# The first layer's output stored from ScalarE's own DMA queue, and the second half of the last block's output copied into a borrowed buffer

## The chip, the cores and the metric

The kernel runs on one core of one Trainium2 chip, the other cores idle. The metric is the device time of one execution in microseconds (us), taken as the median of several runs. The core's engines are TensorE (PE, with its weight loads shown apart as PEld), VectorE (DVE), ScalarE (ACT), GpSimd (POOL, unused here) and SyncE (SP), each with its own instruction queue, and 16 DMA engines that serve the transfers that SP and ACT issue.

## The reference, cut to what matters

```python
def reference(q, k, v, p, moe_w_in, moe_w_out, moe2_w_in, moe2_w_out):
    # attention in two steps; batch 8, heads 8, sequence 576, head size 64, 32 packed rows p
    p_packed = sm_attn(p, k, v)
    out = sm_attn(q, p_packed, p_packed)
    x = out.transpose(0, 2, 1, 3).reshape(4608, 512)
    h = x @ moe_w_in                    # 512 -> 2048
    g = h * np.tanh(softplus(h))        # "Mish"
    y = g @ moe_w_out                   # 2048 -> 512, the first layer's output
    h = y @ moe2_w_in
    g = h - np.tanh(h)
    return g @ moe2_w_out
```

## The kernel before, in words

The 4608 tokens are worked in nine blocks of 512. Block b (0 to 7) holds the last 512 tokens of batch b, and the ninth block ("the rest block", number 8) collects the 64 tokens left over from each of the eight batches. Attention and the first matrix of the first layer are folded together per batch, so for each batch a transposed attention matrix (tiles `a2`, four buffers, two per batch) is multiplied with a per-batch weight (tiles `m`). This gives the inner values of one of 16 feature blocks in a PSUM bank (`bk`, line 821). ACT applies Mish (L826), ACT and DVE split the result into two fp32r halves (L803, L804), and PE multiplies it with the outer weights `wo` into four accumulators (L783). The four accumulators `acc` 0 to 3 are the four blocks of 128 output features, each 128 features by 512 tokens, and every accumulator collects over the 16 feature blocks.

When a block is finished, the function `outputs` empties the accumulators: ACT copies accumulators 0 and 1 into the two halves of a buffer `yv` (L793), a DMA on SP's queue stores it to `y_d` in DRAM (512 KB), and then accumulators 2 and 3 go the same way. There is one buffer `yv`, so the second pair's copy waits until the first pair's store has landed. The next block's sums for an accumulator start only after its copy.

The second layer multiplies by a seven-product scheme for 2x2 blocks (Strassen-Winograd). It works on "supers" of two token blocks each (0 to 3, with super 4 being the rest block alone). `combos` loads the stored `y_d` blocks of a super, forms seven combinations on ACT and DVE (L920, L925, L926) and stores them to `yq_d`. For super 3, which needs block 7, this happens late, through small `x` and `xw` buffers. `load_sup` loads the combinations `yq` of a super back: of seven pairs the first two pairs (four loads of 512 KB) go to the four `a2` buffers, the others to `wo` buffers. `products` makes the seven products for each pair p of feature blocks in `bk` banks (L1047); ACT copies (L1067) and DVE adds (L1072) combine them. `second` computes h - tanh(h) on ACT and DVE (L1104 to L1121, working in the same six `xw` buffers), and PE accumulates the output with L1132.

No order is written out by hand. Every operation is an `Op` with an engine, an assumed duration, a key, the operations that it depends on, and the buffers that it takes and gives back. `Plan.emit` walks a simulated time. Whenever an engine is free it issues the ready operation with the lowest key whose buffers are free. An operation on the pseudo-engine `NONE` issues no instruction. For most kinds of buffer a queue is kept in the order of the keys, and a buffer goes to an operation only when that operation stands at the head of its kind's queue; `a2` is one of these kinds. The order of every engine's instructions therefore depends on these numbers throughout, but is fixed when the program is built.

Of the kernel before, what the change touches and what calls it, by code (L numbers as in the profile page):

```python
# [12 lines left out]
AF = mybir.ActivationFunctionType  # L13
# [5 lines left out]
B, H, S, D, P = 8, 8, 576, 64, 32  # L19
# [3 lines left out]
TB = 512  # L23
# [13 lines left out]
def r(ap):  # L37
    return ap.bitcast(F32R)
# [33 lines left out]
class Plan:  # L72
# [12 lines left out]
    def op(self, eng, dur, fn, key, deps=(), take=(), give=(), table=None):  # L85
        o = Op()
        o.table = table
        o.eng, o.dur, o.fn, o.key = eng, dur, fn, key
        o.takes, o.gives, o.outs, o.ready, o.end = list(take), list(give), [], 0.0, None
        o.wait = 0  # L90
        o.seq = len(self.ops)
        for b in o.gives:
            b.left += 1
        for d in set(x for x in deps if x is not None):
            d.outs.append(o)
            o.wait += 1
        self.ops.append(o)
        return o
# [19 lines left out]
    def emit(self):  # L118
# [3 lines left out]
        free = {e: 0.0 for e in engs}  # L122
# [13 lines left out]
        t, left = 0.0, len(self.ops)  # L136
        while left:
# [7 lines left out]
            while moved:  # L145
                moved = False
                for e in engs:
                    if free[e] > t:
                        continue
                    while pend[e] and pend[e][0][0] <= t:  # L150
                        o = heapq.heappop(pend[e])[2]
# [34 lines left out]
                    o = pick  # L186
# [9 lines left out]
                    if e == "SP":  # L196
                        free[e] = t + 0.475
                        dma_free = max(dma_free, free[e] + 0.65) + o.dur
                        o.end = dma_free + 1.6
                    else:  # L200
                        dur = o.dur
                        if o.table is not None:
                            dur += self.TABLE * (o.table != table)
                            table = o.table
                        if e == "PE":
                            dur = dur if t > self.WARM else 2 * dur
                            pe_end = t + dur
                        free[e] = t + dur
                        o.end = free[e] + self.LAT.get(e, 0.13)
                    for b in o.gives:  # L210
                        b.left -= 1
                        if b.left == 0:
# [14 lines left out]
            t = t2  # L227


def a_cost(n, psum=False, bias=False):  # L230
    return (n / 1.2 + (51 if psum else 93) + (93 if bias else 0)) * 1e-3
# [7 lines left out]
def tile_packed_attention_mish_tanhshrink(  # L239
# [14 lines left out]
    V, A, T, SP = nc.vector, nc.scalar, nc.tensor, nc.sync  # L254
    ctx.enter_context(tc.manual_schedule())
    plan = Plan()
    op = plan.op
# [18 lines left out]
    K = {}  # L276
# [12 lines left out]
    y_d = dr.tile([4, 128, NT], F32, name="y_d")  # L289
# [21 lines left out]
    T0, TA, TR, TP = 9.98, 4.95, 2.75, 10.5  # L311
# [7 lines left out]
    def dma(out, in_, kbytes, key, deps=(), take=(), give=()):  # L319
        return op("SP", kbytes / 350.0, lambda: SP.dma_start(out(), in_()), key, deps, take, give)  # L320
# [161 lines left out]
    a2, a2_rd, fxs = {}, {}, {}  # L482
# [280 lines left out]
    y_st, rest_st = {}, {}  # L763
    g2_last, e_, acc1, gate = {}, {}, {}, []

    def outputs(blk, fc, k0, gv, c0, c1, deps, gives):

        whole = blk == 0 and fc // 2 in F_OUT
        gate.extend([] if gate else deps + [wo_f[fc] if whole else wo_rd[fc]])
        first, last = fc == 0, fc == NFC - 1  # L770
        yv, done = None, None
        for oc in range(4):
            if first and c0 == 0:
                acc1[oc] = Buf(K["acc", oc], [128, 512])
            ac = acc1[oc]

            def f(oc=oc, ac=ac):
                if whole:
                    T.matmul(ac.tile[:, c0:c1], wf[fc // 2].tile[:, fc % 2, oc * 128:(oc + 1) * 128], gv(),
                             start=first and c0 == 0, stop=False, skip_group_check=True)  # L780
                    return
                for i, (wl, gl) in enumerate(PASSES):
                    T.matmul(ac.tile[:, c0:c1], r(wo[fc].tile[:, wl, oc * 128:(oc + 1) * 128]), r(gv(gl)),  # L783
                             start=first and c0 == 0 and i == 0, stop=last and c1 == TB and i == 2,
                             skip_group_check=blk == 0)
            g2_last[oc] = z = op("PE", 2e-3 * ((c1 - c0) / 1.2 + 13) if whole else 3e-3 * ((c1 - c0) / 2.4 + 13), f,
                                 k0 + 2.62 * TA + 0.1 * oc, deps + [wo_f[fc] if whole else wo_rd[fc], g2_last.get(oc)],
                                 [ac] if first and c0 == 0 else [], gives + ([wf[fc // 2]] if whole else []))
            if not last or c1 < TB:
                continue  # L790
            if oc % 2 == 0:
                yv, done = Buf(K["yv"], [128, 2, TB]), []
            done.append(op("ACT", a_cost(TB, True), lambda ac=ac, oc=oc, yv=yv: A.activation(  # L793
                yv.tile[:, oc % 2, :], ac.tile, AF.Copy), k0 + TA, [z] + done, [yv] if oc % 2 == 0 else [], [ac]))
            if oc % 2:
                y_st[blk, oc // 2] = dma(
                    lambda oc=oc: y_d[oc - 1:oc + 1, :, blk * TB:(blk + 1) * TB].rearrange("o p t -> p o t"),
                    lambda yv=yv: yv.tile, 512, k0 + TA, done[1:], give=[yv])

    def split(kf, ev, shape, rd, give):  # L800
        gt = Buf(K["g"], [128, 2] + shape)
# [478 lines left out]
```

## Time and profile before

| what | value |
|---|---|
| median of 3 runs | 1451.32 us (1450.23 to 1454.66) |
| the profiled execution | 1450.54 us, of which the span on the core 1448.7 us |
| PE busy | 1439.0 us, 99% of the span |
| DVE busy | 1027.7 us, 71% |
| ACT busy | 970.3 us, 67% |
| DMA moved | 366.50 MB, 253 GB/s on average |
| granted TensorE clock | 0.998 of full |

Busy time is the time in which an engine had at least one instruction at work. Matmuls overlap and their ends are modelled, so 99% does not say that PE ran at its peak; it says that there was hardly a moment without a matmul in flight. The shares are averages over the whole span, and the stretches differ: the first layer lasts to about 730 us, and the second layer follows, with the two interleaved from about 670 us on.

### The profile page before, as it was taken

Reading aid. Unit: us, or ns where it says so; the run is one execution under the profiler, and the core shown is the slowest. Engines: PE = TensorE matmul, PEld = TensorE weight load, DVE = VectorE, ACT = ScalarE, POOL = GpSimd, SP = SyncE. Lnnn points to the kernel's source line nnn. Section 1 sums busy time; section 2 is a strip of 40 time slices with the busy share of each in tenths; the row PEclk is TensorE's granted clock in tenths of the full one; section 3 lists DMA queues with packets and bytes.
Section 4 is the critical chain, followed back from the end, with each engine's and each line's share of the span. In section 5 each row is a group of like instructions: output and inputs, shape, how many; then the busy total and the mean of one; then the engine's idle time right before and its main releaser. Section 6 shows DMA issues by size and latency. Waiting matters only on the chain.

```text
span 1448.7 us, 23090 instructions
## 1 busy us (share of the span) xinstructions
PE 1439.0 (99%) x8486; PEld 1188.3 (82%) x8486; DVE 1027.7 (71%) x1834; ACT 970.3 (67%) x1833; POOL 0.2 (0%) x4
## 2 busy tenths in 40 slices
PE   8999999999999999999999999999999999999998
PEld 6787888888888788888888888888888888888887
DVE  6996675746575766634699947897488946898575
ACT  6887676856666666644597827776477936776574
POOL 0000000000000000000000000000000000000000
PEclk9999999999999999999999999999999999999999
DMA  9998585857676886959965966579665976566782
GB/s 326 295 340 265 188 288 179 276 183 264 205 231 225 288 296 229 332 200 352 378 224 195 387 230 232 189 265 355 197 208 189 371 260 218 180 206 234 261 300 79
DMA packets 143409, 366.50 MB, mean 253 GB/s; under 512 B 30912, under 2 KB 44608, under 8 KB 138176
## 3 DMA queue, kind: packets, MB, share of 16 engines
q1 hardware_dynamic: 142864, 364.70, 72.2%
q8 instruction: 67, 1.10, 0.3%
q10 hardware_dynamic: 432, 0.33, 0.1%
q14 instruction: 46, 0.38, 0.1%
HBM read 285.28 MB, written 79.69 MB: 252 GB/s over the span
## 4 chain that ended last, share of the span: by engine, by line
PE 93%; DMA 4%; DVE 2%; ACT 1%; issue 0%; SPq 0%; ACTq 0%; DVEq 0%
PE acc L1132 27%; PE acc L783 25%; PE bk L1047 24%; PE bk L821 12%; PE bk L746 2%; DMA st<-in_w1o 1%; DMA st<-in_w1i 1%; PE bk L627 1%; PE bk L654 1%; DMA yq_d<-st 1%; PE bk L600 1%; DMA x<-in_k 0%; PE bk L549 0%; DMA a<-in_k 0%; DMA st<-in_w2o 0%
## 5 line engine op out<-in xcount | busy, mean ns | idle before, releaser
L783 PE MATMUL acc<-g,wo 128*128 128x512 f32 x1680 | 415.0, 393 | 0.1
L1132 PE MATMUL acc<-g,wo 128*128 128x512 f32 x1728 | 410.2, 390 | 0.0
L1132 PEld LDWEIGHTS acc<-g,wo 128*128 128x128 f32 x1728 | 322.3, 188 | 66.3 <-ACT x L1144 0.7
L783 PEld LDWEIGHTS acc<-g,wo 128*128 128x128 f32 x1680 | 305.6, 188 | 70.4 <-issue 14.0
L1047 PE MATMUL bk<-wo,m 128*128 128x512 f32 (+1 forms) x1200 | 267.0, 370 | 0.0
L1047 PEld LDWEIGHTS bk<-wo,m 128*128 128x128 f32 x1200 | 209.9, 188 | 44.6 <-ACT pc L1067 5.3
L821 PEld LDWEIGHTS bk<-a,m 128*128 128x128 f32 x1488 | 210.0, 188 | 14.5 <-issue 3.3
L821 PE MATMUL bk<-a,m 128*128 128x288 f32 x1488 | 219.6, 296 | 0.2
L826 ACT ACTIVATE e<-bk 128x288 f32<-128x288 f32 x256 | 103.2, 408 | 112.3 <-PE bk L821 110.2
L804 DVE TENSOR_TENSOR g<-e,g 128x512 fp32r<-128x512 f32 x140 | 96.2, 689 | 104.3 <-ACT g L803 103.2
L1110 DVE SCALAR_TENSOR_TENSOR xw<-xw,xw 128x512 f32<-128x512 f32 x144 | 99.2, 689 | 19.9 <-ACT xw L1107 19.8
L1047 PE MATMUL bk<-a,m 128*128 128x512 f32 (+1 forms) x480 | 106.1, 368 | 0.0
L1105 ACT ACTIVATE xw<-e,c_qb 128x512 f32<-128x512 f32 x144 | 102.8, 714 | 4.8 <-DVE xw L1110 2.7
L803 ACT ACTIVATE g<-e 128x512 fp32r<-128x512 f32 x140 | 88.1, 632 | 20.4 <-PE acc L783 17.4
L1114 DVE TENSOR_TENSOR tt<-x,tt 128x512 f32<-128x512 f32 x96 | 66.5, 692 | 45.1 <-ACT tt L1109 44.9
L1047 PEld LDWEIGHTS bk<-a,m 128*128 128x128 f32 x480 | 84.8, 188 | 15.7
L1107 ACT ACTIVATE xw<-e 128x512 f32<-128x512 f32 x144 | 89.3, 620 | 0.2 <-DVE x L1116 0.2
L1120 ACT ACTIVATE g<-x 128x512 fp32r<-128x512 f32 x96 | 59.4, 625 | 39.1 <-PE acc L1132 32.8
L1067 ACT ACTIVATE pc<-bk 128x512 f32<-128x512 f32 (+1 forms) x120 | 65.5, 546 | 28.2 <-PE bk L1047 27.9
L1089 ACT ACTIVATE x<-bk 128x512 f32<-128x512 f32 (+1 forms) x40 | 22.1, 552 | 87.0 <-PE bk L1047 87.0
L1121 DVE TENSOR_TENSOR g<-x,g 128x512 fp32r<-128x512 f32 x96 | 66.0, 691 | 14.7 <-ACT g L1120 14.7
L1118 DVE COPY_PREDICATED x<-e,tt 128x512 f32<-128x512 uint32 x96 | 73.0, 761 | 0.8
(145 smaller groups left out, 1482.5 us busy)
## 6 DMA issues: line engine op xcount, KB each, us to landing
wo<-w2o_d SPq DMA_DIRECT2D x144, 512.0 KB, 5.0
m<-w2i_d SPq DMA_DIRECT2D x40, 1024.0 KB, 5.1
m<-w2i_d SPq DMA_DIRECT2D x40, 768.0 KB, 4.5
xw<-w1i_d SPq DMA_DIRECT2D x112, 256.0 KB, 4.2
yq_d<-st SPq DMA_DIRECT2D x42, 512.0 KB, 3.6
wo<-yq_d SPq DMA_DIRECT2D x40, 512.0 KB, 11.0
w2i_d<-x SPq DMA_DIRECT2D x56, 256.0 KB, 2.7
x<-in_v SPq DMA_DIRECT2D x40, 256.0 KB, 5.5
```

Of the source, the lines that this page charges most:

```text
L783: T.matmul(ac.tile[:, c0:c1], r(wo[fc].tile[:, wl, oc * 128:(oc + 1) * 128]), r(gv(gl)), start=first and c0 == 0 and i == 0, stop=last and ...
L803: hi = op("ACT", a_cost(n), lambda: A.activation(r(gt.tile[:, 0]), ev(), AF.Copy), kf + 1.1, rd, [gt])
L804: return gt, op("DVE", v_cost(n), lambda: V.tensor_tensor(out=r(gt.tile[:, 1]), in0=ev(), in1=gt.tile[:, 0], op=ALU.subtract), kf + 1.2, [ ...
L821: T.matmul(h.tile[:, :HALF], r(m.tile[:, fc % 4, kc, wl, :]), r(x.tile[:, kc, al, :]), start=(i == 0), stop=(i == 5))
L826: return op("ACT", a_cost(HALF, True), lambda: A.activation(out(), h.tile[:, :HALF], AF.Mish), k0 - (30.42, 29.7, 2.5)[min(b, 2)], [g1] + ...
L1047: T.matmul(bk.tile[:, :n], r(wv[:, kc, wl, :]), r(y), start=(first and i == 0), stop=(i == 5), skip_group_check=not first)
L1105: p1 = op("ACT", a_cost(TB, False, True), lambda: A.activation(s1.tile, zz.tile, AF.Sigmoid, bias=c_qb, scale=Q_L), k0 + 0.1, [sq, act2[0] ...
L1107: p2 = op("ACT", a_cost(TB), lambda: A.activation(s2.tile, zz.tile, AF.Tanh, scale=Q_T), k0 + 0.15, [sq, act2[0]], [s2])
L1110: q = op("DVE", v_cost(TB), lambda: V.scalar_tensor_tensor(out=s1.tile, in0=s1.tile, scalar=Q_E, in1=s2.tile, op0=ALU.add, op1=ALU.mult), ...
L1114: d = op("DVE", v_cost(TB), lambda: V.tensor_tensor(out=tt.tile, in0=h.tile, in1=tt.tile, op=ALU.subtract), k0 + 1.2, [th])
L1118: q = op("DVE", 0.645, lambda: V.copy_predicated(h.tile, zz.tile.bitcast(U32), tt.tile), k0 + 1.4, [q, d, k], give=[zz, tt])
L1132: T.matmul(ac.tile, r(w.tile[:, wl, oc * 128:(oc + 1) * 128]), r(gt.tile[:, gl, :]), start=(first and i == 0), stop=(last and i == 2))
```

## The change

Three things change, all around the emptying of the accumulators.

1. The store of a pair to `y_d` is issued by ACT, right behind the second copy of the pair, and no longer by SP. All 18 stores are moved. In the plan ACT's second copy is 0.4 us longer, and a `NONE` operation of 4.5 us stands for the store.
2. In block 7 (`blk == B - 1`) the second pair is copied to an `a2` buffer, so that it need not wait for `yv`. Its copy has the key `k0 - 30` in place of `k0 + TA`.
3. `Plan.emit` no longer keeps `NONE` busy during such an operation, so that several can be under way at once.

```diff
@@ Plan.emit
-                        free[e] = t + dur
-                        o.end = free[e] + self.LAT.get(e, 0.13)
+                        free[e] = t + dur * (e != "NONE")
+                        o.end = t + dur + self.LAT.get(e, 0.13)
@@ outputs
             if oc % 2 == 0:
-                yv, done = Buf(K["yv"], [128, 2, TB]), []
-            done.append(op("ACT", a_cost(TB, True), lambda ac=ac, oc=oc, yv=yv: A.activation(
-                yv.tile[:, oc % 2, :], ac.tile, AF.Copy), k0 + TA, [z] + done, [yv] if oc % 2 == 0 else [], [ac]))
+                spare = blk == B - 1 and oc
+                yv, done = Buf(K["a2" if spare else "yv"], [128, 2, TB]), []
+
+            def copy(ac=ac, oc=oc, yv=yv):
+                A.activation(yv.tile[:, oc % 2, :], ac.tile, AF.Copy)
+                if oc % 2:
+                    A.dma_start(y_d[oc - 1:oc + 1, :, blk * TB:(blk + 1) * TB].rearrange("o p t -> p o t"), yv.tile)
+            done.append(op("ACT", a_cost(TB, True) + 0.4 * (oc % 2), copy, k0 - 30 if spare else k0 + TA, [z] + done,
+                           [yv] if oc % 2 == 0 else [], [ac]))
             if oc % 2:
-                y_st[blk, oc // 2] = dma(
-                    lambda oc=oc: y_d[oc - 1:oc + 1, :, blk * TB:(blk + 1) * TB].rearrange("o p t -> p o t"),
-                    lambda yv=yv: yv.tile, 512, k0 + TA, done[1:], give=[yv])
+                y_st[blk, oc // 2] = op("NONE", 4.5, lambda: None, k0 + TA, done[1:], give=[yv])
```

Since the plan's times change, the order of instructions changes on every engine, here and there in the first layer and above all around the passage to the second layer. The lines behind the change move by three or four (L1047 is L1051 in the changed kernel, L1132 is L1136). The numbers behind a name count the buffers as they are made and differ between the two programs.

SP's queue as the loads of super 0's first combinations (`a<-yq_d`) stand in the kernel before, two far ahead and two before block 7's first store (`y_d<-yv`):

```order
L320 DMA a_2_6854<-yq_d 128x1024
L320 DMA a_3_6861<-yq_d 128x1024
...
L320 DMA rest_d<-e_7419 256x1x64
L320 DMA a_0_7520<-yq_d 128x1024
L320 DMA a_1_7526<-yq_d 128x1024
L320 DMA rest_d<-e_7487 256x1x64
L320 DMA m_7536<-w2i_d 128x1536
L320 DMA e_7544<-rest_d 128x1024
L320 DMA e_7561<-rest_d 128x1024
L320 DMA y_d<-yv_7575 128x2x512
```

The same place of SP's queue in the changed kernel:

```order
L320 DMA rest_d<-e_7415 256x1x64
L320 DMA m_7520<-w2i_d 128x1536
L320 DMA rest_d<-e_7483 256x1x64
L320 DMA e_7536<-rest_d 128x1024
L320 DMA e_7553<-rest_d 128x1024
L320 DMA a_3_7579<-yq_d 128x1024
L320 DMA a_0_7585<-yq_d 128x1024
L320 DMA a_1_7589<-yq_d 128x1024
L320 DMA e_7602<-rest_d 128x1024
L320 DMA wo_7613<-yq_d 128x1024
L320 DMA x_7622<-y_d 128x512
L320 DMA a_2_7639<-yq_d 128x1024
```

The first pair of loads has moved down by about 30 rows to the second, behind the two loads of the rest block (`e<-rest_d`), and the fourth load, `a_2`, stands behind the loads of `y_d`. The stores of `y_d` have left this queue.

ACT's queue in the changed kernel at the end of block 7, with the borrowed buffer `a_2` (L796 is the copy, L798 the store):

```order
L796 ACTIVATE yv_7567<-acc_0_6977 128x512
L796 ACTIVATE yv_7567<-acc_0_6987 128x512
L798 DMA y_d<-yv_7567 128x2x512
L796 ACTIVATE a_2_7577<-acc_0_6994 128x512
...
L796 ACTIVATE a_2_7577<-acc_0_7014 128x512
L798 DMA y_d<-a_2_7577 128x2x512
```

The store of the first pair no longer stands between the two pairs of copies as a wait, and the same buffer `a_2` is what the fourth load of `yq_d` above fills next.

PE's queue at the passage in the kernel before, from pair 2's fifth product on; `acc` with L1132 is the second layer's output, and one row is half of a product of the seven-product scheme:

```order
L1047 MATMUL bk_8163<-wo_7747,m_7988 128x512 x3
L1047 MATMUL bk_8163<-wo_7792,m_7988 128x512 x3
L1047 MATMUL bk_8129<-wo_7811,m_7988 128x512 x3
L1047 MATMUL bk_8129<-wo_7832,m_7988 128x512 x3
L1132 MATMUL acc_0_8222<-g_8190,wo_7902 128x512 x3
L1132 MATMUL acc_0_8230<-g_8190,wo_7902 128x512 x3
L1047 MATMUL bk_8129<-wo_7857,m_7988 128x512 x3
L1047 MATMUL bk_8129<-wo_7878,m_7988 128x512 x3
```

In the changed kernel, from the fourth product of pair 2 on (`m_8019` is pair 3):

```order
L1051 MATMUL bk_8106<-wo_7657,m_7773 128x512 x3
L1051 MATMUL bk_8106<-wo_7679,m_7773 128x512 x3
L1051 MATMUL bk_8164<-a_3_7579,m_8019 128x512 x3
L1051 MATMUL bk_8164<-a_0_7585,m_8019 128x512 x3
L1051 MATMUL bk_8184<-a_1_7589,m_8019 128x512 x3
L1051 MATMUL bk_8184<-a_2_7639,m_8019 128x512 x3
L1051 MATMUL bk_8136<-wo_7735,m_7984 128x512 x3
L1051 MATMUL bk_8136<-wo_7780,m_7984 128x512 x3
L1051 MATMUL bk_8106<-wo_7809,m_7984 128x512 x3
L1051 MATMUL bk_8106<-wo_7829,m_7984 128x512 x3
L1136 MATMUL acc_0_8227<-g_8206,wo_7900 128x512 x3
```

Two products of pair 3 have been brought forward, ahead of pair 2's fifth product and of the first output matmuls.

PE's queue where block 7 ends and the rest block begins, in the changed kernel (the first product of the second layer, then the rest block's first sums L783, then the second product):

```order
L1051 MATMUL bk_7670<-a_3_7579,m_7198 128x512 x3
L1051 MATMUL bk_7670<-a_0_7585,m_7198 128x512 x3
L783 MATMUL acc_0_7581<-g_7611,wo_696 128x512 x3
L783 MATMUL acc_0_7591<-g_7611,wo_696 128x512 x3
L783 MATMUL acc_0_7598<-g_7611,wo_696 128x512 x3
L1051 MATMUL bk_7706<-a_1_7589,m_7198 128x512 x3
L1051 MATMUL bk_7706<-a_2_7639,m_7198 128x512 x3
```

In the kernel before the second product stands right behind the first; here nine matmuls of the rest block stand between them.

## Rows read from the trace of the kernel before

**Rows 1.** The page: span, busy time, and busy tenths in 40 slices.

```profile
span 1448.7 us, 23090 instructions
PE 1439.0 (99%) x8486; PEld 1188.3 (82%) x8486; DVE 1027.7 (71%) x1834; ACT 970.3 (67%) x1833; POOL 0.2 (0%) x4
...
PE   8999999999999999999999999999999999999998
...
PEclk9999999999999999999999999999999999999999
```

**Rows 2.** The page: the chain that ended last, by engine.

```profile
PE 93%; DMA 4%; DVE 2%; ACT 1%; issue 0%; SPq 0%; ACTq 0%; DVEq 0%
```

**Rows 3.** Waits, whole span: us in total, times, longest.

```profile
ACT yv L793 <- DMA y_d<-yv: 3.4, 3, 2.4
...
PEld acc L783 <- ACT yv L793: 1.5, 4, 0.5
...
PEld bk L821 <- ACT yv L793: 0.8, 1, 0.8
```

**Rows 4.** The one store that ACT issues already, by its line.

```profile
L1148 ACTq DMA_DIRECT2D out_t<-x x1: 350/350/350, 1445.4 to 1445.4; - x1
```

**Rows 5.** DMA issues, whole span: count, size, median us from issue to landing.

```profile
wo<-yq_d SPq DMA_DIRECT2D x40, 512.0 KB, 11.0
...
y_d<-yv SPq DMA_DIRECT2D x18, 512.0 KB, 4.8
...
a<-yq_d SPq DMA_DIRECT2D x16, 512.0 KB, 7.2
```

**Rows 6.** Timeline of ACT at block 7's end: start, us, engine, line [idle before].

```profile
658.19 1.28 ACT L793 ACTIVATE yv<-acc 128x512 f32<-128x512 f32 x2
660.23 0.63 ACT L803 ACTIVATE g<-e 128x512 fp32r<-128x512 f32 x1 [0.76 <-PE acc L783]
663.29 1.09 ACT L793 ACTIVATE yv<-acc 128x512 f32<-128x512 f32 x2 [2.43 <-DMA y_d<-yv]
```

**Rows 7.** Timeline of SP's queue, 560 to 682 us.

```profile
580.42 1.96 SPq L320 DMA_DIRECT2D a<-yq_d  x2
...
651.27 1.11 SPq L320 DMA_DIRECT2D a<-yq_d  x2
...
656.75 0.79 SPq L320 DMA_DIRECT2D e<-rest_d  x2
```

**Rows 8.** Windows: PE, PEld, DVE, ACT, POOL busy, PEclk, DMA share, GB/s.

```profile
640.00:660.00 20.00, 20.00 (x105) 17.38 (x104) 4.75 (x7) 8.84 (x16) 0.00 (x0) 1.00 0.52 177
660.00:680.00 20.00, 20.00 (x90) 16.54 (x89) 10.56 (x17) 9.37 (x17) 0.00 (x0) 1.00 0.95 337
680.00:700.00 20.00, 20.00 (x90) 16.57 (x89) 8.31 (x13) 7.65 (x13) 0.00 (x0) 1.00 1.04 412
700.00:720.00 20.00, 20.00 (x90) 16.57 (x89) 11.81 (x20) 9.90 (x18) 0.00 (x0) 1.00 0.99 358
720.00:740.00 20.00, 20.00 (x90) 16.57 (x89) 19.77 (x36) 19.97 (x38) 0.00 (x0) 1.00 0.78 276
740.00:760.00 20.00, 20.00 (x89) 16.25 (x89) 19.88 (x36) 16.86 (x32) 0.00 (x0) 1.00 0.64 204
```

**Rows 9.** Timeline of PE, 655 to 690 us: the first products.

```profile
670.91 2.88 PE L1047 MATMUL bk<-a,m 128*128 128x512 f32 x12
673.63 2.88 PE L783 MATMUL acc<-g,wo 128*128 128x512 f32 x12
```

**Rows 10.** Timeline of ACT, 700 to 745 us: the second layer's first sigmoid.

```profile
713.37 0.72 ACT L1105 ACTIVATE xw<-e,c_qb 128x512 f32<-128x512 f32 x1 [1.70 <-DMA yq_d<-xw]
```

**Rows 11.** Timeline of DVE, 700 to 745 us: an add and the first output operand.

```profile
725.85 0.69 DVE L1072 TENSOR_TENSOR x<-bk,pc 128x512 f32<-128x512 f32 x1
...
729.22 0.69 DVE L1121 TENSOR_TENSOR g<-x,g 128x512 fp32r<-128x512 f32 x1
```

**Rows 12.** Timeline of PE, 700 to 770 us: pair 2's products, the first output.

```profile
722.59 2.88 PE L1047 MATMUL bk<-a,m 128*128 128x512 f32 x12
725.31 5.60 PE L1047 MATMUL bk<-wo,m 128*128 128x512 f32 x24
730.75 1.52 PE L1132 MATMUL acc<-g,wo 128*128 128x512 f32 x6
```

## The prediction

> **What bounds the kernel now.** I read the page first. PE has a matmul in flight for 99% of the span, its tenths are 9 in all but the first and last slice, and the granted clock is full throughout [rows 1]. The chain that ended last runs through PE for 93% [rows 2]. So the work of PE, whose matmuls the change neither adds nor removes, is the time, and only what makes PE stand still or removes such standing can move it. PE's non-busy time is 1448.7 - 1439.0 = 9.7 us in all, and the tenths put what shows of it at the two ends. That is a ceiling on any gain, far above what the change could reach.
>
> Then I asked the waits whom the copies hold up. ACT waited 3.4 us in three places for a store of `yv`, and PE's weight loads waited 1.5 + 0.8 = 2.3 us for ACT's copies [rows 3]. These are the waits that the change can remove. With matmuls in flight for 99% of the time, not all of the 2.3 us can have been lost.
>
> Last I cut the passage between the layers into windows of 20 us [rows 8]. From 660 to 720 us the DMA engines are full (shares 0.95, 1.04, 0.99, up to 412 GB/s), and from 720 to 740 us DVE (19.77 of 20) and ACT (19.97 of 20) are full as well; DVE stays full to 760. PE is busy through all of it. Here lateness in the supply can't be caught up quickly, and this is where the order of SP and PE changes most.
>
> **The stores on ACT's queue.** One issue took ACT 0.350 us in the only store of this kind that it has [rows 4]; 18 stores make 6.3 us of ACT. SP is relieved of 18 issues, but it is not the engine that is short. ACT is 67% busy [rows 1], so I cost 16 of the issues at nothing: what hides them is PE's queue of work while ACT idles. If that cover is gone at every one, 16 x 0.35 = 5.6 us is the upper end; the lower end is minus the 2.3 us of PE's waits for copies, if all of those go. I take 0, since the waits that remain in place of the old ones are of the same size. A store issued by ACT stands behind its own copy and in front of the next Mish, whose result PE needs; it is 0.35 us late for it. The last two stores, the rest block's, come in the stretch in which ACT is full, so I charge them: 0.7 us (0 to 0.7).
>
> The page "DMA: Bandwidth & Descriptors" of the Trainium skill, section "Issuing engines are not separate DMA queues", says that transfers issued by different engines run on the same 16 DMA engines and that another issuer only saves sequencer time. By that rule the transfers themselves gain nothing by the move, and the sum stays as it is; the share of 1.04 between 680 and 700 us [rows 8] agrees that there is no idle DMA engine to be found in the passage.
>
> **Block 7's second pair.** Before, its copies start at 663.29 us after 2.43 us of waiting for the first store [rows 6]; with a buffer of their own they start about 2.4 us earlier. Nothing on PE waited for them there (PE is busy 20.00 of 20 in those windows [rows 8]), so this gains 0.
>
> **The borrowed buffer's price: one late load.** The fourth `yq` load goes to the same `a2` buffer and must wait for the second pair's store. Copies of 1.09 us from 660.9 end at 662.0, and with 4.8 us to land [rows 5] the store is done at 666.8. The load then lands 7.2 us later by the median of its kind, at 674.0, or 11.0 us later by that of the `wo` loads from the same tensor, at 677.8 [rows 5]. PE reads it in the second half of the second product. In the order of the changed kernel that follows the first product (670.91 plus 1.36, half of the 12 matmuls' pitch of 2.72 in [rows 9]), nine matmuls of L783 (2.04) and half a product (0.68): at 675.0. So PE waits between 0 and 2.8 us. I take 0.5, nearer to the row of the load's own kind.
>
> **Its second price: loads moved into the full stretch.** This one shows only in the order. The copy into `a2` stands at the head of that buffer's queue, so the plan gives no `a2` buffer to a load before it. Two loads that were issued at 580.42 us, and two issued at 651.27 us when the DMA share was 0.52 [rows 7, 8], now all stand behind the rest block's loads of 656.75 us [rows 7]. Two loads of 512 KB (0.524 MB) at 412 GB/s are 2 x 1.27 = 2.5 us of the DMA engines; all four are 5.1 us. They push back everything behind them in a queue that is full for 60 us: the loads of `y_d`, super 3's combinations and their stores from `xw`. Late next is the second layer: its first sigmoid needs an `xw` buffer and already waits 1.70 us for such a store, until 713.37 [rows 10]. So it moves by d = 2.5 to 5.1 us.
>
> What covers d? The first output matmul starts at 730.75 [rows 12], and its operand is ready at 729.22 + 0.69 = 729.91 [rows 11]: 0.84 us of slack. The changed order puts two products of pair 3 in front, 2.72 us more, so that matmul itself is covered up to d = 3.56. But the second of these two needs a bank that DVE's add empties, at 725.85 + 0.69 = 726.54 before [rows 11], 729.0 to 731.6 after. PE arrives there five products behind 722.59, at 722.59 + 5 x 1.36 = 729.39 [rows 12]. So with d = 2.5 there is no wait, with d = 5.1 there are 2.2 us. Products brought forward are also missing later, while DVE is full to 760 us and can't catch up. In the end PE loses between 0 (all covered) and 5.1 - 0.84 = 4.3 us; I take the middle, 2.1.
>
> **Reordering elsewhere.** The other shifts on PE exchange whole groups of matmuls in the first layer, with the same groups on either side; they cost nothing as long as their operands are ready, and PE's tenths leave no sign of waiting for them to remove.
>
> **Sum.** 0 + 0.7 + 0 + 0.5 + 2.1 = 3.3 us. Against the profiled execution's 1450.54 us that is 1453.8. That execution lies 0.78 us under the median of the runs, so the median should go from 1451.32 to about 1454.6 us, plus 0.23%. About 0.3% (4.4 us) is what a measurement of this kernel can tell from no change; its three runs alone span 1450.23 to 1454.66. So the forecast is: no difference that can be told, leaning to the slow side.
>
> **The rivals.**
> - *Slower.* All four loads fall into the full DMA stretch and d is 5.1 us. Then the whole 4.3 us reach PE, with the 0.7 of the exposed issues and 0.5 of the late load 5.5 us: 1456.8 us. It decides from d of about 4 us on (4 - 0.84 + 0.7 + 0.5 = 4.4). For it speaks the full DMA, DVE and ACT of 660 to 760 us [rows 8], and that two further costs can join: issues on ACT that PE feels in the first layer (up to 5.6), and a later fourth load (2.8). Against it: two of the four loads were at 651.27 before, shortly ahead of the stretch, and the 640 to 660 window has room for them.
> - *Nothing shows.* d is 2.5, the products brought forward cover it, and the issues on ACT are hidden: 0.5 + 0.7 at the most, 1451.3 to 1452.5 us. For it: PE's busy share and that PE has waited for neither ACT nor DVE there.
> - *Faster.* A store on a queue of its own need not stand behind SP's backlog, lands earlier, and so ACT's waits of 3.4 us for `yv` shrink and PE's 2.3 us go [rows 3]. (The same page of the Trainium skill, section "Queues, rings and completion order", says that each DMA engine takes turns between queue rows, which is this rival's mechanism; no run here shows it yet.) Without other costs the time is 1451.32 - 2.3 = 1449.0 us, still within 0.3%. To pass the bound of 4.4 us it would have to remove waits that the trace does not have.
>
> **How the numbers follow.** The forecast, a loss of 1.2 to 4.4 us, has 0.48; slower, 0.33; nothing shows, 0.12; the store's gain within the bound, 0.04; faster beyond it, 0.03. So faster 0.03, the same 0.64, slower 0.33. The extremes of the terms are 1449.0 (minus 2.3) and 1464.7 us (5.6 + 0.7 + 2.8 + 4.3). Eight in ten lie from 1451.0 to 1459.5: the low end leaves out the store's gain, the high end the case in which several issues on ACT are felt as well. The likeliest case's own range is 1452.5 to 1455.7.
>
> **What would show it.** Right: PE's busy share lower by some tenths of a per cent; a wait of PE for a load of `yq_d` near 675 us, and for DVE's adds (L1072) between 728 and 800 us; the first sigmoid (L1105) later than 713.37 + 2.5; all four `a<-yq_d` loads issued after 650 us; 18 stores of 0.35 us in ACT's queue. Wrong: the first sigmoid at its old time, so that the moved loads cost nothing; or PE gaps spread over the first layer's blocks, each behind an ACT store, which would make the issues the cause and not the buffer; or PE gaps at none of these places with a time off by more than 4 us.

## The result and the profile after

| | kernel before | changed kernel |
|---|---|---|
| median, 5 runs each on one chip | 1453.53 us (1450.23 to 1454.66) | 1466.45 us (1465.08 to 1469.82) |
| the profiled execution, its span | 1450.54, 1448.7 us | 1467.53, 1465.7 us |

The ratio of the means is 1.0098, 95% interval [1.0079, 1.0117]: the change costs about 1%. The time lies above the predicted range, and above the 1464.7 us that the prediction gave as the extreme of its terms. The two profiled spans differ by 17.0 us, more than the medians (12.9), because the profiled execution of before lies 3.0 us under this median and that of after 1.1 us over it.

The page of the changed kernel, beside [rows 1, 2]: PE is busy 4.4 us longer in a span that is 17 us longer, and PE's share of the chain that ended last has gone from 93% to 80%.

```profile
span 1465.7 us, 23074 instructions
PE 1443.4 (98%) x8486; PEld 1188.3 (81%) x8486; DVE 1025.6 (70%) x1834; ACT 972.2 (66%) x1833; POOL 0.2 (0%) x4
...
PE 80%; DMA 9%; DVE 6%; ACT 3%; issue 1%; SPq 0%; ACTq 0%; DVEq 0%
```

Windows tell where PE stands still. Before, the three stretches of the first layer (first column the stretch, third PE's busy time):

```profile
60.00:240.00 180.00, 179.88 (x1418) 147.13 (x1417) 126.61 (x250) 132.76 (x267) 0.00 (x0) 1.00 0.76 256
240.00:440.00 200.00, 199.87 (x1488) 164.18 (x1488) 129.15 (x248) 135.85 (x262) 0.00 (x0) 1.00 0.70 234
440.00:640.00 200.00, 199.70 (x1418) 166.63 (x1417) 121.31 (x206) 129.88 (x250) 0.00 (x0) 1.00 0.77 271
```

The changed kernel, the same three, the passage in two pieces, and the second layer:

```profile
60.00:240.00 180.00, 178.67 (x1338) 144.45 (x1336) 126.63 (x246) 131.56 (x263) 0.00 (x0) 1.00 0.76 252
240.00:440.00 200.00, 198.23 (x1517) 163.28 (x1517) 125.75 (x243) 133.11 (x258) 0.00 (x0) 1.00 0.67 222
440.00:640.00 200.00, 196.32 (x1415) 161.72 (x1414) 123.02 (x213) 130.65 (x250) 0.00 (x0) 1.00 0.76 266
640.00:700.00 60.00, 56.56 (x280) 48.17 (x279) 18.80 (x29) 24.20 (x44) 0.00 (x0) 1.00 0.74 264
700.00:760.00 60.00, 58.72 (x258) 47.99 (x257) 36.19 (x61) 35.52 (x65) 0.00 (x0) 1.00 0.87 325
760.00:1440.00 680.00, 679.92 (x3120) 563.33 (x3120) 539.68 (x933) 465.66 (x855) 0.00 (x0) 1.00 0.70 247
```

In the first layer PE idled 0.12 + 0.13 + 0.30 = 0.55 us before and 1.33 + 1.77 + 3.68 = 6.78 us after; 3.44 + 1.28 = 4.72 us come at the passage and nothing behind it. The granted clock is full in all of them. PE's lateness, the start of the n-th matmul of a run minus that of the n-th of before, gives the same picture and takes in matmuls that only run slower. It is the measure for the experiments too (us, at times of the kernel before; one profiled execution each):

| kernel | at 70 us | 157 | 286 | 445 | 643 | 731 | 777 | end |
|---|---|---|---|---|---|---|---|---|
| changed kernel | 1.6 | 3.1 | 5.4 | 8.3 | 11.2 | 16.8 | 16.9 | 16.9 |
| e1_sp_issue | -0.2 | 0.8 | 4.3 | 5.4 | 9.1 | 15.9 | 16.7 | 16.7 |
| e2_act_issue | 1.2 | 0.9 | 2.2 | 2.7 | 1.1 | 2.0 | 2.7 | 2.6 |
| e3_no_borrow | 0.6 | 1.4 | 4.5 | 6.7 | 11.8 | 13.9 | 14.4 | 14.2 |
| e6_borrow_only | 3.3 | 2.6 | 3.0 | 2.9 | 2.6 | 2.6 | 4.8 | 4.8 |
| e8_charge_dma | -0.4 | 0.6 | 1.6 | 1.6 | 0.5 | 0.5 | 7.7 | 7.5 |
| e12_charge_no_borrow | 0.1 | 0.1 | 0.8 | 0.9 | 1.1 | 4.3 | 4.5 | 4.5 |

What differs by 70 us is no effect of the change: the first store is issued at 115 us, and the two programs' orders on PE part only at the 709th matmul, behind that point. In e6, whose order on PE is that of before up to the 4012th matmul, it is 3.3 us, so differences of this size say nothing by themselves; nor is the profiled execution always near its median (e1's and e15's are their slowest, 4 and 5 us above it, e16's is its fastest, 4 us below). So of the 16.9 us about 9.6 arise in the first layer, 6.6 of them idle time in eleven gaps of 0.15 to 1.16 us, and 5.6 between 643 and 731 us.

The waits of the changed kernel (us in total, times, longest), beside [rows 3]. ACT waits for stores of `yv` no longer than before over the whole span, though in the first layer alone its waits have grown from 0.96 to 2.64 us. PE's weight loads wait for ACT's copies 5.1 us in place of 1.5, and two waits are new or longer (3.9 us for `a<-yq_d`, and 3.2 us for DVE's adds against 1.3):

```profile
PEld acc L783 <- ACT yv L796: 5.1, 6, 1.6
...
PEld bk L1051 <- DMA a<-yq_d: 3.9, 1, 3.9
...
PEld bk L1051 <- DVE x L1076: 3.2, 8, 1.3
...
ACT yv L796 <- DMA y_d<-yv: 3.3, 4, 1.6
```

Pieces of the chain that ended last (start, us). Four of them belong to the stores and to the borrowed buffer's load; before, no store of `y_d` was among its 200 longest pieces:

```profile
520.52 7.44 DMA y_d<-yv
...
672.75 11.06 DMA y_d<-a
683.88 5.87 DMA a<-yq_d
...
737.00 6.08 DMA y_d<-yv
```

The plan took 4.5 us for each of these stores. What a late one does is seen at 528 us on ACT:

```profile
525.75 0.63 ACT L807 ACTIVATE g<-e 128x512 fp32r<-128x512 f32 x1
527.98 0.60 ACT L796 ACTIVATE yv<-acc 128x512 f32<-128x512 f32 x1 [1.60 <-DMA y_d<-yv]
528.60 1.28 ACT L830 ACT_TABLE_LOAD   x1
```

and on PE at the same moment:

```profile
526.51 0.96 PE L825 MATMUL bk<-a,m 128*128 128x288 f32 x6
528.63 0.96 PE L783 MATMUL acc<-g,wo 128*128 128x512 f32 x3 [1.16 <-ACT yv L796]
```

The plan let the copy go as soon as it thought the buffer free, ACT stood at it for 1.60 us with the table load and the Mish queued behind, and PE, whose next sum needs the emptied accumulator, stood still.

Most of the first layer's gaps are not of this kind. Four of them stand behind ACT's copies, 3.30 us in all. At 203 and 528 us (1.42 us of PE's idle time) ACT had waited for a store. At 287 us it had waited 1.82 us for a load of the second layer's weights, which are prepared during the first layer, and only 0.08 for a store; at 606 us, 1.63 for a load of `y_d`. ACT and PE at 287 us:

```profile
285.55 0.65 ACT L340 ACTIVATE st<-st 128x512 f32<-128x512 f32 x1 [1.82 <-DMA st<-in_w2o]
...
286.93 2.33 PE L783 MATMUL acc<-g,wo 128*128 128x512 f32 x9 [1.13 <-ACT yv L796]
```

The other seven wait for other work of ACT and DVE, and the chain there goes through stores of prepared weights (`w2i_d<-x`, `w2o_d<-so`) and loads. So a store that lands late is one way in which the new order loses time, and not the only one.

The stores by their line (ns min/median/max of the issue; landing in us min/median/max, the store from the borrowed buffer with them), beside [rows 4, 5]:

```profile
L798 ACTq DMA_DIRECT2D y_d<-yv x17: 365/366/412, 115.4 to 744.7; - x17
...
DMA to landing us min/median/max: 2.7/5.8/11.1
```

### The profile page after: what moved, and what is told of

Same layout as the page of the kernel before. It is cut to its first block, busy times and chain, and to the rows that moved or that the text cites. A ratio compares the mean times of both kernels' runs of the same rounds, so it can differ in the third digit from the quotient of the medians.

```text
span 1465.7 us, 23074 instructions
## 1 busy us (share of the span) xinstructions
PE 1443.4 (98%) x8486; PEld 1188.3 (81%) x8486; DVE 1025.6 (70%) x1834; ACT 972.2 (66%) x1833; POOL 0.2 (0%) x4
## 4 chain that ended last, share of the span: by engine, by line
PE 80%; DMA 9%; DVE 6%; ACT 3%; issue 1%; SPq 0%; ACTq 0%; DVEq 0%
PE acc L1136 26%; PE bk L1051 22%; PE acc L783 19%; PE bk L825 9%; DMA w2o_d<-so 2%; DMA st<-in_w1o 2%; PE bk L746 2%; DMA w2i_d<-x 1%; DMA y_d<-yv 1%; DMA y_d<-a 1%; DMA st<-y_d 1%; PE bk L627 1%; ACT e L830 0%; PE bk L654 0%; DMA a<-in_k 0%
## 5 line engine op out<-in xcount | busy, mean ns | idle before, releaser
L783 PE MATMUL acc<-g,wo 128*128 128x512 f32 x1680 | 416.9, 393 | 3.6 <-ACT yv L796 3.3
L1136 PE MATMUL acc<-g,wo 128*128 128x512 f32 x1728 | 409.8, 390 | 0.0
L1136 PEld LDWEIGHTS acc<-g,wo 128*128 128x128 f32 x1728 | 322.4, 188 | 66.3 <-ACT x L1148 0.7
L783 PEld LDWEIGHTS acc<-g,wo 128*128 128x128 f32 x1680 | 305.3, 188 | 76.4 <-issue 15.1
L1051 PE MATMUL bk<-wo,m 128*128 128x512 f32 (+1 forms) x1200 | 267.1, 370 | 0.5 <-ACT pc L1071 0.4
L1051 PEld LDWEIGHTS bk<-wo,m 128*128 128x128 f32 x1200 | 209.8, 188 | 45.3 <-ACT pc L1071 5.1
L1051 PE MATMUL bk<-a,m 128*128 128x512 f32 (+1 forms) x480 | 107.0, 368 | 4.3 <-DMA a<-yq_d 3.4
L1051 PEld LDWEIGHTS bk<-a,m 128*128 128x128 f32 x480 | 84.7, 188 | 20.7 <-DMA a<-yq_d 3.9
```

The lines of the kernel that those rows point to most:

```text
L1051: T.matmul(bk.tile[:, :n], r(wv[:, kc, wl, :]), r(y), start=(first and i == 0), stop=(i == 5), skip_group_check=not first)
L1136: T.matmul(ac.tile, r(w.tile[:, wl, oc * 128:(oc + 1) * 128]), r(gt.tile[:, gl, :]), start=(first and i == 0), stop=(last and i == 2))
```

## The experiments

Theory A: the issues on ACT make PE wait. Theory B: the borrowed buffer does. Theory C: neither; the plan's new numbers for the store change the order of the whole first layer, and that order waits. All times are against the kernel before on the same chip (medians 1451.4 to 1452.2 us there), and the ratios are of the means.

| kernel | median (lowest to highest) us | ratio to before, interval |
|---|---|---|
| e1_sp_issue | 1463.12 (1462.64 to 1467.2) | 1.0085 [1.0065, 1.0104] |
| e2_act_issue | 1454.13 (1451.14 to 1457.47) | 1.0019 [1.0009, 1.003] |
| e3_no_borrow | 1464.32 (1462.81 to 1465.15) | 1.0086 [1.007, 1.0101] |
| e6_borrow_only | 1454.41 (1449.79 to 1455.56) | 1.0007 [0.9995, 1.0019] |
| e8_charge_dma | 1458.42 (1457.38 to 1460.33) | 1.005 [1.0037, 1.0062] |
| e9_no_0p4 | 1467.38 (1466.15 to 1469.04) | 1.011 [1.0094, 1.0125] |
| e4_est7p5 | 1461.08 (1460.38 to 1462.21) | 1.0067 [1.0055, 1.008] |
| e10_before_0p4 | 1453.44 (1450.2 to 1456.73) | 1.0013 [1.0001, 1.0024] |
| e12_charge_no_borrow | 1455.01 (1452.12 to 1459.33) | 1.0021 [1.0009, 1.0032] |
| e14_before_no_charge | 1455.03 (1452.65 to 1458.77) | 1.0027 [1.0016, 1.0038] |
| e15_end_behind_loads | 1460.28 (1459.11 to 1465.2) | 1.0057 [1.0043, 1.0071] |
| e16_booked_end_4p5 | 1464.7 (1460.43 to 1473.08) | 1.0097 [1.0069, 1.0124] |

**e1_sp_issue.** The changed kernel's order on PE, ACT, DVE and of SP's other transfers, with the stores issued by SP at the place of the second copy.

```diff
-                    A.dma_start(y_d[...], yv.tile)
+                    SP.dma_start(y_d[...], yv.tile)
```

> The changed kernel with every instruction on PE, ACT and DVE in the same order, but its 18 stores of y_d issued by SP at the place where the plan puts the second copy. Theory 'order' (the loss comes from the order that the plan now makes, with 4.5 us assumed for a store, and from the borrowed buffer): as slow as the changed kernel, 1464 to 1469 us, with PE gaps of about 1 us in the first layer at the second pair's copies and the wait for a<-yq_d near 690 us. Theory 'issue' (the stores in ACT's queue hold up ACT, and that reaches PE in every block): the first layer's gaps of about 8 us go, 1457 to 1460 us.

Nearly the whole loss stays (1.0085 against 1.0098). Three stores stand in the chain here too, although ACT issues none:

```profile
519.14 7.09 DMA y_d<-yv
597.33 5.71 DMA y_d<-yv
...
733.31 9.01 DMA y_d<-yv
```

**e2_act_issue.** The kernel before in its own order, with ACT issuing each store behind the copy; the plan still books it on SP.

```diff
... (the copy with its A.dma_start, as in the changed kernel)
-                y_st[blk, oc // 2] = dma(..., 512, k0 + TA, done[1:], give=[yv])
+                y_st[blk, oc // 2] = op("SP", 512 / 350.0, lambda: None, k0 + TA, done[1:], give=[yv])
```

> The kernel before with every instruction on PE, ACT, DVE and SP in the same order, but its 18 stores issued by ACT right behind the copy. Theory 'order': as fast as before, within 1.5 us of it. Theory 'issue': slower by the first layer's gaps, 5 to 9 us.

It costs 0.19% (0.0019 x 1452 = 2.8 us). With e1 this leaves theory A about a fifth of the loss.

**e3_no_borrow and e6_borrow_only.** The changed kernel without the borrowed buffer, and the kernel before with it alone (stores on SP).

```diff
# e3
-                spare = blk == B - 1 and oc
+                spare = False
# e6, in the kernel before
-                yv, done = Buf(K["yv"], [128, 2, TB]), []
+                spare = blk == B - 1 and oc
+                yv, done = Buf(K["a2" if spare else "yv"], [128, 2, TB]), []
...
-                ... AF.Copy), k0 + TA, [z] + done, ...
+                ... AF.Copy), k0 - 30 if spare else k0 + TA, [z] + done, ...
```

> The changed kernel without the borrowed buffer: block 7's second pair goes to yv as in the other blocks; the order is that of the changed kernel up to the end of block 7. Theory 'two parts': the wait for a<-yq_d (3.9 us) and the gaps near 745 us (1.6 us) go, and the first layer's gaps of some 8 us stay: 1459 to 1462 us. Rival 'all in the first layer': the passage finds another wait, 1464 to 1467 us. Rival 'all in the borrowed buffer': back at the time of before, 1451 to 1455 us.

> The kernel before with the borrowed buffer alone: stores on SP as before, the same order as before up to the end of block 7. Theory 'two parts': slower than before by the late load and the passage, 4 to 6 us: 1457 to 1459 us, with a PE wait for a<-yq_d of 3 us or more. Rival 'all in the first layer': within 1.5 us of before.

The borrowed buffer alone costs nothing that can be told (1.0007; the interval, -0.7 to 2.8 us, takes in zero), and the loss stays without it (1.0086). Theory B falls as the cause of the loss. e6 is also the prediction's buffer terms in the old order: its four `a<-yq_d` loads are all issued behind 662 us, the first sigmoid moves from 713.37 [rows 10] to 727.28, and PE, which had no wait for `yq_d`, loses 2.2 us between 731 and 777 us (4.8 - 2.6). ACT and PE:

```profile
727.28 0.72 ACT L1106 ACTIVATE xw<-e,c_qb 128x512 f32<-128x512 f32 x1
...
738.55 3.23 PE L1048 MATMUL bk<-wo,m 128*128 128x512 f32 x12 [0.91 <-ACT pc L1068]
742.46 1.66 PE L1048 MATMUL bk<-a,m 128*128 128x512 f32 x6 [0.69 <-ACT x L1090]
```

The waits of e3 show what the borrow had spared: ACT's waits for stores of `yv` are 12.0 us in place of 3.3.

```profile
ACT yv L796 <- DMA y_d<-yv: 12.0, 8, 4.7
```

So theory C is left, and its numbers were taken one by one: (a) the 0.4 us on the second copy, (b) the store's 1.46 us of DMA time, which the plan before booked and so moved later loads back, (c) the store's end, which the plan before reckoned behind the loads in flight and the new one sets to 4.5 us. A rival (d): any order other than that of before costs, and the more so the more it differs.

**e8_charge_dma.** Both (b) and (c) as before (the condition on the key leaves out another `NONE` operation, which is no store).

```diff
                         o.end = t + dur + self.LAT.get(e, 0.13)
+                        if e == "NONE" and o.key > 0 and dur > 0:
+                            dma_free = max(dma_free, t + 1.125) + 512 / 350.0
+                            o.end = dma_free + 1.6
```

> The changed kernel, but its plan again books each store's 512/350 us of DMA time, as the plan before did, so that loads behind a store are thought to land that much later; stores stay on ScalarE. e1_sp_issue put about 12 of the 14 us on the order that the plan makes and not on who issues the store; three of the plan's numbers changed, and this run undoes one. If the missing booking made the bad order: 1455 to 1458, and the delay of the PE by the end of the first layer's block 7 falls from about 11 to about 3 us. If the 0.4 us on the second copy made it: 1463 to 1467. If the 4.5 us as the store's end made it: 1463 to 1467, since with the booking a store's end lies at 4.2 us or later, much as now. If any departure from the order before costs, whichever number makes it: 1457 or more.

The first layer's loss is gone: PE is 0.5 us late at 643 us against 11.2, and the ratio falls by 0.48%. (The third part of the change, `NONE` no longer kept busy, is still in e8, so it did not make that loss by itself.) Then PE loses 7.2 us between 731 and 777 us, which no theory had foreseen. The timeline of PE there:

```profile
733.98 1.52 PE L1054 MATMUL bk<-wo,m 128*128 128x512 f32 x6
739.35 5.34 PE L1054 MATMUL bk<-wo,m 128*128 128x512 f32 x12 [3.85 <-ACT pc L1074]
```

and of ACT:

```profile
733.99 0.58 ACT L799 ACTIVATE yv<-acc 128x512 f32<-128x512 f32 x1
...
734.98 0.58 ACT L799 ACTIVATE yv<-acc 128x512 f32<-128x512 f32 x1
...
735.60 0.37 ACTq L801 DMA_DIRECT2D y_d<-yv  x1
...
738.72 0.57 ACT L1074 ACTIVATE pc<-bk 128x512 f32<-128x512 f32 x1
```

The copies and the store of the rest block, and five operations of the second layer behind them, stand on ACT ahead of the `pc` copy that PE waits for, in a stretch in which ACT and DVE have no room. The copies and the store are not enough by themselves: in e12 below they stand right ahead of a `pc` copy too (738.70 us), and PE loses 0.2 us between 731 and 777 us.

**e9_no_0p4 and e10_before_0p4.** (a) alone taken out of the changed kernel, and alone put into the kernel before.

```diff
# e9
-            done.append(op("ACT", a_cost(TB, True) + 0.4 * (oc % 2), copy, ...
+            done.append(op("ACT", a_cost(TB, True), copy, ...
# e10, in the kernel before
-            done.append(op("ACT", a_cost(TB, True), lambda ...
+            done.append(op("ACT", a_cost(TB, True) + 0.4 * (oc % 2), lambda ...
```

> The changed kernel, but the plan books nothing for the store's issue on the second copy (a_cost alone in place of a_cost + 0.4). If the 0.4 us made the bad order: 1455 to 1458. If the missing booking of DMA time made it: 1463 to 1467. If the 4.5 us did: 1463 to 1467. If any departure costs: 1457 or more.

> The kernel before (stores on SyncE, booked as before), with only the 0.4 us added to the second copy in the plan; nothing is issued by ScalarE. Its order is that of before up to PE's product 1701 of 7608. If the 0.4 us made the bad order: 1458 to 1464. If the booking or the 4.5 us made it: 1451 to 1454, no change. If any departure from the order before costs: 1456 or more.

Without (a) the changed kernel is no better (1.011), and (a) alone costs 0.13%: (a) is not the cause. e10 also speaks against (d): its order on PE differs from that of before at 276 of 7606 places (counted by the names read and written, without their numbers). Among the first 4054 matmuls, up to the second layer's first product, the order differs at 264 places in the changed kernel, 267 in e8, 246 in e12 and 234 in e10, and PE is 11.2, 0.5, 1.1 and 0.3 us late at 643 us. So it is not how much the order differs, but how.

**e4_est7p5.** (c) made longer, nothing else.

```diff
-                y_st[blk, oc // 2] = op("NONE", 4.5, lambda: None, k0 + TA, done[1:], give=[yv])
+                y_st[blk, oc // 2] = op("NONE", 7.5, lambda: None, k0 + TA, done[1:], give=[yv])
```

> The changed kernel, but its plan takes a store to end 7.5 us after the copy in place of 4.5 (the 17 stores landed after a median of 5.8 us and at most 11.1). If the too short end made the bad order (second copies and their buffers planned before the buffer is free): 1455 to 1459, and ScalarE's waits for y_d<-yv at the copy (3.3 us in 4 waits) fall to under 1. If the booking or the 0.4 us made it: 1463 to 1468 with those waits gone or not. If any departure costs: 1457 or more.

The ratio falls by 0.31%, ACT's waits for stores of `yv` are gone from the list, and of the stores only the borrowed buffer's is left in the chain:

```profile
667.02 11.79 DMA y_d<-a
...
679.23 6.16 DMA a<-yq_d
```

**e12_charge_no_borrow.** e8 with `spare = False`.

> e8_charge_dma without the borrowed buffer (spare = False); its order is that of e8 up to the end of block 7. In e8 PE was 0.5 us late at 731 us and 7.7 us late at 777 us, with a wait of 3.9 us for pc behind two copies and a store on ScalarE at 734 to 736 us. If the borrowed buffer makes this loss at the passage between the layers: about 1451.5 to 1455 and a delay at 777 us under 3. If the copies and the store on ScalarE make it, or the order whatever it is: 1457 to 1460, delay 6 to 8 us.

Without the borrowed buffer the loss behind 731 us is gone. There is 3.2 us of another instead, at the end of block 7, since the second pair now waits for the first pair's store. ACT:

```profile
668.13 1.08 ACT L799 ACTIVATE yv<-acc 128x512 f32<-128x512 f32 x2 [6.21 <-DMA y_d<-yv]
```

PE:

```profile
668.78 6.44 PE L786 MATMUL acc<-g,wo 128*128 128x512 f32 x27 [2.77 <-ACT yv L799]
```

At 1.0021 it costs what e2 costs, in an order that differs from that of before at 288 places on PE. So (d) falls, and the borrowed buffer costs 1.0050 - 1.0021 = 0.29% here, against 0.07% by itself in e6 and 1.0098 - 1.0086 = 0.12% in the changed kernel (e3).

**e14, e15, e16.** (b) alone dropped from the kernel before; (c) alone undone in the changed kernel; (b) alone undone in the changed kernel.

```diff
# e14, in the kernel before, for these stores
-                        dma_free = max(dma_free, free[e] + 0.65) + o.dur
-                        o.end = dma_free + 1.6
+                        start = max(dma_free, free[e] + 0.65)
+                        o.end = start + o.dur + 1.6
+                        dma_free = start + o.dur if not o.store else dma_free
# e15, in place of the two lines of e8
+                            o.end = max(dma_free, t + 1.125) + 512 / 350.0 + 1.6
# e16, in place of the two lines of e8
+                            dma_free = max(dma_free, t + 1.125) + 512 / 350.0
```

> The kernel before, stores on SyncE, with one number of the plan changed: a store no longer moves on the time at which the DMA engines are thought free for later loads (its own end is still reckoned behind the loads ahead of it). If the loads behind a store, thought to land too early, made the bad order of the first layer: a delay of 6 to 11 us by 643 us and 1458 to 1464. If the store's own end did (fixed at 4.5 us in the changed kernel, whatever is queued ahead of it): under 2 us of delay, 1451 to 1454.

> The changed kernel, but the plan reckons a store's end behind the loads that the DMA engines still have (the later of that time and 1.125 us, plus 1.46 and 1.6), as before; the store itself is still not booked for the loads behind it. One half of e8. If the fixed end of 4.5 us made the first layer's bad order: a delay of 0 to 3 us by 643 us (e8: 0.5, the changed kernel: 11.2), total 1453 to 1460 with what the passage adds. If the missing booking did: 9 to 12 us by 643 us, 1462 to 1467.

> The changed kernel, but the plan books each store's 1.46 us for the loads behind it and keeps the store's own end at a fixed 4.5 us. The other half of e8. If the missing booking made the first layer's bad order: a delay of 0 to 3 us by 643 us, total 1453 to 1460. If the fixed end did: 9 to 12 us by 643 us, 1462 to 1467. If each has a part: both this run and e15_end_behind_loads lie between, at 4 to 8 us.

By the ratios (c) is the larger half: undone alone it takes the ratio from 1.0098 to 1.0057, while undoing (b) alone shows no gain (1.0097, runs from 1460 to 1473 us). Dropping (b) alone from the kernel before costs 0.27%, with PE 3.5 us late at 643 us, between the two outcomes that were expected. The lateness at 643 us says less: 7.1 us in e15 and 4.0 in e16, but the profiled executions were e15's slowest (1465.2) and e16's fastest (1460.43). That both together make the first layer's loss is shown by e8 and e12; how they share it is not settled. No version was faster than the kernel before, and e6 alone can't be told from it.

## Why the prediction was wrong

**Reordering elsewhere: the step that failed.** It put the shifts in the first layer at nothing "as long as their operands are ready", and took PE's full tenths as the evidence that they would be. But those tenths belonged to the old order. In the new one 9.6 of the 15.3 us arose in the first layer (11.2 - 1.6, and 16.9 - 1.6): PE waited there for ACT's copies, for DVE and for ACT's other work, and e8 shows that the plan's numbers for the store made that order. The diff showed both numbers: 4.5 us as a fixed end, against stores that took 4.8 us by the median [rows 5] and up to 11.1 here, and a DMA booking that was gone. I read them as bookkeeping for the moved issue and gave no term to them; the "Slower" rival had the sign, but its place was the passage. The range's high end, 1459.5, was worked out from ACT's issues and the passage alone, so a loss of this size in the first layer had no place in it.

**16 issues on ACT: 0.** Mis-sized: e2 measured 2.8 us (interval 0.09% to 0.3%, 1.3 to 4.4 us) for all 18, where the two terms for them made 0.7; it lies inside the bounds of -2.3 to +5.6. The named sign of the issues as the cause, gaps spread over the first layer, did come, but e1 has them without a store on ACT. That sign could not tell the issue from the order. The rest block's two exposed issues (0.7) were not measured apart.

**Block 7's second pair: 0.** It did start at once, at 671.11 us right behind the first store. That it gains nothing held for the old order; in e12 the pair without the second buffer costs PE 2.77 us.

**The late load: 0.5 us.** Right in place and mechanism, mis-sized: PE waited 3.44 us, past the upper end of 2.8.

```profile
685.51 0.84 PE L1051 MATMUL bk<-a,m 128*128 128x512 f32 x3
689.79 0.96 PE L1051 MATMUL bk<-a,m 128*128 128x512 f32 x3 [3.44 <-DMA a<-yq_d]
```

PE came at 686.35 us, the forecast 675.0 plus its lateness of 11.2. The store and the load behind it took 11.06 + 5.87 = 16.9 us, where the prediction had 4.8 + 7.2 = 12.0: the store's landing was the wrong size, and its end is what the load waits for. The kind's median was taken for a store that shares the DMA engines with three loads issued beside it:

```profile
669.04 1.45 SPq L320 DMA_DIRECT2D a<-yq_d  x3
...
683.88 0.32 SPq L320 DMA_DIRECT2D a<-yq_d  x1
```

In e8 and e16 the same store took 10.6 and 10.7 us and PE had no wait for the load, so this price is one of the order as well.

**Loads in the full stretch: 2.1 us.** All four stood behind 650 us, and PE lost 1.9 us more (14.9 to 16.8) with waits for DVE's adds near 745 us, as foreseen. In e6, where the buffer and the loads that it moves are the only difference, PE lost 2.2. But the d of 2.5 to 5.1 us that the term was worked out from was too small. The first sigmoid moved from 713.37 [rows 10] to this:

```profile
737.46 0.72 ACT L1109 ACTIVATE xw<-e,c_qb 128x512 f32<-128x512 f32 x1 [0.50 <-ACT yv L796]
```

That is 24.1 us, 9.2 more than PE's own lateness of 14.9 there. Beyond PE's lateness it moved by 8.6 to 11.3 us in every kernel with the borrowed buffer, and by 0.2 to 1.9 in e2, e3, e10, e12 and e14, which are without it. In e6, e8 and e16 the figure is 11.27 in all three, and in e6 the sigmoid stands behind a `pc` copy that had waited for PE: it is the plan's order that puts it there, and not only full DMA engines. DVE's full stretch, which the term builds on, began later as well: DVE was busy 7.03 of 20 us from 720 to 740, and 19.22 and 20.00 in the next two windows of 20. So the size of this term came right with a d of twice the size and more cover than was reckoned, which is luck in part. In the changed kernel the chain there also goes through the rest block's store (6.08 us in place of 4.5) and the copy at 743.10 us behind it, which the prediction did not have; how the 1.9 us divide was not tried.

**The faster rival.** It hoped that a store on a queue of its own would land earlier. Against the same order, stores on ACT's queue landed no earlier: a median of 5.3 us in e2 against 4.8 before [rows 5], and 5.6 in the changed kernel against 4.1 in e1. (One profiled execution each; with stores on SP the median was 4.7 in e14 and 5.4 in e10, so the first of these differences is within what the order does.)

```profile
y_d<-yv ACTq DMA_DIRECT2D x17, 512.0 KB, 5.6
...
y_d<-a ACTq DMA_DIRECT2D x1, 512.0 KB, 11.1
```

The Trainium skill's page "DMA: Bandwidth & Descriptors", section "Issuing engines are not separate DMA queues", says that another issuer saves only sequencer time; these runs agree that the transfers gained nothing.

Along one path the ratios add up: the plan's two numbers 0.48% (changed kernel less e8), borrowed buffer 0.29% (e8 less e12), and issue 0.19% (e2) for the 0.21% that e12 is left with. Each has an interval of 0.1% or more, and the parts are not independent: along another path the borrowed buffer is 0.12% (changed kernel less e3).

## What to carry to other kernels

In a kernel whose order comes from a planner, every number that the planner is given is part of the change: compare what it assumed of a moved transfer (its end, what it queues behind, the bandwidth it takes from others) before and after, and set that against the measured landings. A full engine in the old trace is no evidence for another order, and a price worked out in the old order (here the borrowed buffer's, which e6 bears out) holds for the old order. To tell an instruction's own cost from that of the order it causes, run the old order with the new instruction and the new order with the old one.

## What the runs showed of the hardware

A DMA issue costs ACT a little more than its row: in the changed kernel the issue at 744.73 us lasted 0.37, and ACT was idle 0.44 us before its next instruction, against 0.35 for the one row of before [rows 4]. ACT's timeline:

```profile
744.12 0.59 ACT L796 ACTIVATE yv<-acc 128x512 f32<-128x512 f32 x1
744.73 0.37 ACTq L798 DMA_DIRECT2D y_d<-yv  x1
745.15 0.72 ACT L1109 ACTIVATE xw<-e,c_qb 128x512 f32<-128x512 f32 x1 [0.44 <-ACT yv L796]
```

A gap on PE can cost more than itself. In e8, PE idled 3.85 us before 739.35, and the granted clock was 0.56 from 740 to 745 us, close to the 1.2 GHz level; the 12 matmuls behind the gap took 5.34 us, where 12 took 2.88 before [rows 9]:

```profile
735.00:740.00 5.00, 1.15 (x5) 0.64 (x4) 5.00 (x11) 4.56 (x10) 0.00 (x0) 0.76 0.93 365
740.00:745.00 5.00, 4.68 (x12) 3.28 (x10) 5.00 (x10) 3.40 (x7) 0.00 (x0) 0.56 0.30 99
745.00:750.00 5.00, 4.63 (x20) 3.85 (x21) 4.05 (x8) 5.00 (x11) 0.00 (x0) 1.00 0.77 269
```

In the changed kernel PE idled 3.44 us at 686 us and the clock stayed at 1.00; in e1 it idled 3.37 us before 746 us and the clock was 0.66 from 745 to 750. In e12 2.77 us before 668.78 left it at 1.00, and in e16, after 2.12 us before 736.99, it was 0.81 from 740 to 745. So the length of the last gap alone does not tell; what else does was not tried.
